# Row-halved projections in a four-layer attention kernel: one job in two half-wide banks instead of two jobs in two whole banks

## The chip, the cores and the metric

The kernel runs on one core of a Trainium2 chip. Its metric is the device time of one execution in microseconds (us), lower is better. Matrix products run on TensorE (PE, with its weight loads listed as PEld), elementwise work on VectorE (DVE), ScalarE (ACT) and GpSimd (POOL), and SyncE (SP) issues nearly all transfers (DMAs). Products land in PSUM, which has eight banks of 512 fp32 columns for 128 partitions; from there DVE or ACT copies them to SBUF.

## What is computed

An input of 2048 tokens by 512 features passes four residual layers, A, B, A, B. Each one normalizes its input, projects it, attends with 32 heads of 16 features, and projects back. All is fp32.

```python
def _A_ref(x, wqkv, w_phi, wo):        # linear attention on learned features
    q, k, v = qkv[0], qkv[1], qkv[2]
    phi_q = concatenate([softmax(q @ w_phi), softmax(-q @ w_phi)]); phi_k likewise
    kv = phi_k^T v;  z = sum phi_k
    return ((phi_q kv) / (phi_q z + 1e-6)) @ wo

def _B_ref(x, wq, wk, wv, wo, beta):   # N = 4 segments of L = 512 tokens
    for s in range(N):
        qs, ks, vs = q[:, :, s], k[:, :, s], v[:, :, s]
        p = softmax(qs ks^T * scale + causal mask)
        a_mem = (phi(qs) M) / (phi(qs) z + 1e-6)      # phi(t) = t + 1 if t > 0 else exp(t)
        o = sigmoid(beta) * a_mem + (1 - sigmoid(beta)) * (p vs)
        M = M + phi(ks)^T vs;  z = z + sum phi(ks)
    return o @ wo

x = x + _A_ref(_layernorm(x), ...); x = x + _B_ref(_layernorm(x), ...); and both once more
```

## The kernel before

The products that need accuracy are made of fp32r operands split in a high and a low part: hi·hi, hi·lo and lo·hi, three matmuls for each 128 rows of the contraction. A projection of one token block or one column block of 128 contracts over 512 features, so over four chunks `kc`.

**Layer B** (class `LayerB`) takes some 440 us of the span each time, and the change is there alone. Its method `steps` writes out the order of work by hand. It runs through 160 *slots* `k`, five for each of the 32 half blocks `m` (`R = 5`; a segment has eight half blocks, a half block has four heads). I call the five slots of a half block a *turn* and name a slot by its place, "slot 2.3" being slot 3 of turn 2 of a segment, as the tables do. In a slot come, in this order on PE: one piece of `attend` (the logits of the current half block, bank pair `lg`, then one exponential over 1024 columns on ACT, then POOL's causal mask), one piece of `maxima` (the logits of a later half block, banks `mx` and `my`, reduced by DVE to row maxima `mxs`), in slots 0 and 2 `weighted` (the product with v, bank `pv`), and then whatever the table has for the slot. `held` keeps PE's instructions in the order of the program, and `Ordered` does so for the other engines and for SP.

The tables `FIRST` (segment 0), `GAPS` (segments 1 and 2), `LAST` and `FINAL` (segment 3 of the two B layers) say what a slot does. `u/2` stands for two *units* of the projections, `max` for `put_maxima` (a PE transpose of `mxs` into a `g` bank, ACT's copy `mt`, and its DMA into row 63 of the queries that the logits read, `e<-mt` in the profile), `ln` for one 128-token block of the next segment's normalized input turned by four PE transposes (`columns`), `t` for four transposes of the features of k (`tokens`), `m` for the memory's update, `a` for its reading, `x` and `w` for loads. A `~` puts DVE's part of an end off to the next slot.

PSUM is full: two banks for `lg`, one each for `mx`, `my` and `pv`, and **three `g` banks** (`G = 3`), which the projections, the transposes and the memory's products share.

**Projections in the steps.** `PAIRS` names them two by two: q and k of a column block, v of a token block, and the output product `out` of the segment before. `pair` runs both jobs of a name pair at once, each in a whole `g` bank of 512 columns. The array is split in two halves of 64 rows; in one step job 0 uses rows 0 to 63 and job 1 rows 64 to 127 of the same chunk, and after the four chunks they swap ("turned"). A unit is one step: three matmuls of 64 rows by 512 columns for each job, eight units to the pair. Since the other half of the rows then adds to the same bank, the first matmul after the swap waits for a tick: `passed` has DVE copy one element (`beat`) after the last matmul of the half before, at the start of the next slot. Eight projections per B layer, early ones, are done whole by `whole` with all 128 rows (`BEFORE`); 52 per layer go through `pair`.

When a pair is complete, each job's end runs. For q and k that is `projected`: ACT copies the high part out of PSUM (tile `ta`), DVE subtracts it from the bank to give the low part (`ta<-g,ta`), and, where the features are wanted (q in segments 1 to 3, k in segments 0 to 2), ACT reads the bank again for exp (`self.later`, so a slot later) and for relu (another slot later in segments 0 and 1); POOL then makes the features of both. The bank is free after the last of these reads. For v, ACT copies the bank (`v<-g`); for `out`, DVE adds it to the residual (`xr<-g,xr`).

Weights of q and k come from DRAM by SP in halves of 64 rows into a ring of two places (`queue_w`). `stack` lays high and low parts of q and k out as operands of the logits with six DMAs (`e<-ta`): in slot 0 of a turn for `m < 4` and in slot 2 for later half blocks, three turns ahead.

Of the kernel before, what the change touches and what calls it, by code (L numbers as in the profile page):

```python
# [7 lines left out]
F32 = mybir.dt.float32  # L8
# [69 lines left out]


FIRST = """  # L80
0.1 u/2 | 0.2 max u/2 | 0.3 u/2 | 0.4 u/2~
1.0 m0 t1 u/1 | 1.1 u/2 | 1.2 max u/1 w | 1.3 u/2 | 1.4 u/2~
2.0 m1 ln | 2.1 ln~ | 2.2 max ln | 2.3 ln~ w | 2.4 w
3.0 t2 | 3.1 u/2 w | 3.2 max | 3.3 u/2 | 3.4 u/2
4.0 m2 | 4.1 u/2 load | 4.2 max | 4.3 u/2 | 4.4 u/2
5.0 n t3 | 5.1 u/2 | 5.2 max | 5.3 u/2~ n | 5.4 u/2
6.0 m3 n | 6.1 u/2 | 6.2 max | 6.3 u/2 | 6.4 a0+ u/2~
7.0 n t0+ u/1 | 7.1 u/2 | 7.2 n max u/1 | 7.3 u/2 n | 7.4 u/2~
# [12 lines left out]
LAST = """  # L101
0.0 u/1 | 0.1 u/2 | 0.2 n max u/1 | 0.3 u/2 n | 0.4 a1 u/2~ n
1.0 n u/1 | 1.1 u/2 n | 1.2 n max u/1 | 1.3 u/2 n | 1.4 u/2~ n
2.0 ln | 2.2 ln max | 2.3 u/3 | 2.4 a2 u/2 x0 x1 pre
3.0 ln u/1 | 3.1 u/1 | 3.2 ln max u/1 | 3.3 pre u/2 x2 | 3.4 u/2
4.1 x3 u/2 | 4.2 max | 4.3 pre u/2 | 4.4 a3 v/2
5.1 v/2 | 5.2 max v/1 | 5.3 fin v/1 | 5.4 v/2 pre
6.1 v/2 | 6.2 max | 6.3 fin v/2 | 6.4 v/2
7.1 pt p/3 v/2 | 7.2 v/2 | 7.3 fin v/2 p/3 | 7.4 p/3
"""  # L110
FINAL = """
0.0 u/1 | 0.1 u/2 | 0.2 max u/1 | 0.3 u/2 | 0.4 a1 u/2~
1.0 u/1 | 1.1 u/2 | 1.2 max u/1 | 1.3 u/2 | 1.4 u/2~
2.2 max | 2.3 u/3 pre | 2.4 a2 u/2 x0
3.0 x1 u/1 | 3.1 u/1 | 3.2 max u/1 | 3.3 pre u/2 x2 | 3.4 u/2
4.1 x3 u/2 | 4.2 max | 4.3 pre u/2 | 4.4 a3
5.2 max | 5.3 fin | 5.4 pre
6.2 max | 6.3 fin
# [9 lines left out]
def interleave_kernel(ctx, tc, x_in, a_wqkv, a_wphi, a_wo, b_wq, b_wk, b_wv, b_wo, b_beta,  # L128
# [15 lines left out]
    def nm(s):  # L144
        uid[0] += 1
        return f"{s}_{uid[0]}"
# [84 lines left out]
    def dma(out, in_):  # L231
        return sync.dma_start(out=out.bitcast(F32), in_=in_.bitcast(F32))
# [798 lines left out]
    class LayerB:  # L1031
# [22 lines left out]
        def values(self, s):  # L1054

            v = sp.tile([P, 4, VROW], F32, tag="v", bufs=2, name=nm("v"))
            self.vv[s] = [v]
            for j in (0, 2 * VW - 1):
                pool.memset(v[:, :, 0 : H * VW].rearrange("p t (h e) -> p t h e", e=2 * VW)[:, :, :, j : j + 1], 1.0)
            pool.memset(v[:, :, H * VW : H * VW + 1], 1.0)  # L1060
            hT = self.hT[s]
            for t in (0, 3, 1, 2):
                def end(po, t=t):
                    act.copy(v[:, t, 0 : H * VW].rearrange("p (h e) -> p h e", e=2 * VW)[:, :, 1 : 2 * VW - 1],
                             po.rearrange("p (h e) -> p h e", e=2 * DH))
                yield (lambda a, kc, t=t: hT[a][:, kc, t * P : (t + 1) * P], lambda b, kc: self.wv[b][:, kc, :],
                       end, lambda h: None)

        def queue_w(self, n, h):

            if n < len(self.wnext):
                m, c = self.wnext[n]
                rows = slice(64 * h, 64 * h + 64)
                dma(self.ring[rows, n % 2], wqk[m][rows, c])

        def whole(self, job):

            lhs, rhs, end, used = job
            po = PS("g", G)
            yield from mm3(po, lhs, rhs)  # L1080
            used(0)
            used(1)
            end(po)
            yield

        def pair(self, names, make):

            jobs = [make(n) for n in names[:2]]  # L1090
            po = [PS("g", G) for _ in jobs]
            order = [(0, 0), (0, 1), (0, 2), (0, 3), (1, 0), (1, 1), (1, 2), (1, 3)]
            if names[2:]:
                order = [(0, 0), (0, 1), (0, 2), (1, 0), (1, 1), (1, 2), (1, 3), (0, 3)]
            halves = [[0, 0], [0, 0]]
            for step, (turned, kc) in enumerate(order):
                for n, (a, b) in enumerate(((0, 0), (0, 1), (1, 0))):
                    for j, (lhs, rhs, _, _) in enumerate(jobs):
                        h = (j + turned) % 2
                        rows = slice(64 * h, 64 * h + 64)  # L1100
                        i = mm(po[j], lhsT=lhs(a, kc)[rows], rhs=rhs(b, kc)[rows], start=(step == 0 and n == 0),
                               stop=(step == 7 and n == 2), tile_position=(64 * h, 0))
                        if step and n == 0 and turned != order[step - 1][0]:
                            marked(i)
                        if j and n == 2 and step < 7 and turned != order[step + 1][0]:
                            last_half[0] = i
                for j, job in enumerate(jobs):
                    h = (j + turned) % 2
                    halves[j][h] += 1
                    if halves[j][h] == NC:  # L1110
                        job[3](h)
                if step == 7:
                    for p, job in zip(po, jobs):
                        job[2](p)
                yield

        def proj(self, s, c, m):

            d, hT = self.st.setdefault((s, c), {}), self.hT[s]
            n = self.wused  # L1120
            w = self.ring[:, n % 2]
            self.wused += 1
            return (lambda a, kc: w[:, a, kc, :], lambda b, kc: hT[b][:, kc, :],
                    lambda pp: self.projected(d, s, m, pp), lambda h: self.queue_w(n + 2, h))

        def projected(self, d, s, m, pp):

            hi, lo = d["part", m] = [T2("ta1", TA, F32R) for _ in range(2)]
            act.copy(hi, pp)
            wait(lambda: dve.tensor_tensor(out=lo, in0=pp, in1=hi.bitcast(F32), op=SUB))  # L1130
            if not (s == 0 if m == 0 else s == NSEG - 1):
                e = d["phi", m] = T2("tb2", TB2)
                r = T2("tb3", 2)

                def first():
                    act.activation(e, pp, AF.Exp)

                def second():
                    act.activation(r, pp, AF.Relu)
                    pool.tensor_scalar(e, e, 1.0, None, op0=MIN)  # L1140
                    pool.tensor_tensor(out=e, in0=e, in1=r, op=ADD)
                self.later += [first, (lambda: self.later.append(second)) if s < 2 else second]

        def at(self, k, f, *a):

# [351 lines left out]

        def out(self, s):
            for t in range(4):
                def end(po, t=t):  # L1500
                    def added():
                        x = self.xq.pop(0)
                        dve.tensor_tensor(out=x, in0=po, in1=x, op=ADD)
                        sync.dma_start(out=self.xdst[4 * s + t], in_=x)
                    wait(added)
                yield (lambda a, kc, t=t: self.oT[s, kc][a][:, t * P : (t + 1) * P],
                       lambda b, kc: self.wo[b][:, kc, :], end, lambda h: None)

        def early(self):

# [20 lines left out]
        def opening(self):  # L1531
            self.wo = []
            self.wnext = [(m, c) for _ in range(NSEG) for c in range(NC) for m in range(2)]
            self.ring = wp.tile([P, 2, 2, NC, P], F32R, tag="w4", bufs=1, name=nm("wqk"))
            self.wused = 0
            for n in range(2):
                for h in range(2):
                    self.queue_w(n, h)
                yield
            self.wv = []  # L1540
            yield from bring(self.wv, "bwv")
# [7 lines left out]
        def steps(self, side, after, table_end):  # L1549
# [20 lines left out]

            def units():
                for s in range(NSEG):
                    for names in PAIRS[0 if s == 0 else 1 if s < NSEG - 1 else 2]:
                        yield from self.pair(names.split(), lambda name: job(name, s))
            units = units()

            def do(what, s, k):
# [186 lines left out]
```

## Time and profile before

| | us |
|---|---|
| median of 3 runs | 1469.98 (1467.95 to 1474.74) |
| the profiled execution | 1470.59 |
| its span | 1468.9 |
| busy of the span: PE / DVE / ACT / POOL | 1381.1 / 976.4 / 816.2 / 736.9 |

One execution was profiled. The span runs from its first to its last instruction; the profiled execution's own time is 1.7 us longer and lies 0.6 us above the median. Busy time is the union of an engine's instructions; matmuls are pipelined and their ends are modelled, so PE's busy time holds some waiting too. "PEclk" is the share of TensorE's full clock that was granted.

The two B layers' steps lie at 293 to 735 us and at 1012 to 1455 us of the span. The matmuls of the row-halved projections are listed by shape as 64*128 (rows by columns of weights), 64x512 (rows by columns that stream).

### The profile page before, as it was taken

Reading aid. Unit: us, or ns where it says so; the run is one execution under the profiler, and the core shown is the slowest. Engines: PE = TensorE matmul, PEld = TensorE weight load, DVE = VectorE, ACT = ScalarE, POOL = GpSimd, SP = SyncE. Lnnn points to the kernel's source line nnn. Section 1 sums busy time; section 2 is a strip of 40 time slices with the busy share of each in tenths; the row PEclk is TensorE's granted clock in tenths of the full one; section 3 lists DMA queues with packets and bytes.
Section 4 is the critical chain, followed back from the end, with each engine's and each line's share of the span. In section 5 each row is a group of like instructions: output and inputs, shape, how many; then the busy total and the mean of one; then the engine's idle time right before and its main releaser. Section 6 shows DMA issues by size and latency. Waiting matters only on the chain. (4 is left out here: it accounts for less than half of the span.)

```text
span 1468.9 us, 35919 instructions
## 1 busy us (share of the span) xinstructions
PE 1381.1 (94%) x13318; PEld 998.7 (68%) x13318; DVE 976.4 (66%) x3088; ACT 816.2 (56%) x1244; POOL 736.9 (50%) x1073
## 2 busy tenths in 40 slices
PE   9999999998999899988999999999999988998998
PEld 7787787765666565655568887876566666666654
DVE  5766896875666566567646778958666665666673
ACT  5655455355775675556644434543567656755653
POOL 1678764134564555544524456531355456644543
PEclk9999999998999999999999999999999999999998
DMA  5469285555665575657640106754655566655551
GB/s 190 128 218 360 81 274 171 161 134 144 155 142 155 143 167 135 156 147 209 174 153 33 55 23 201 224 169 119 169 145 136 135 164 163 147 145 140 145 167 60
DMA packets 136766, 225.46 MB, mean 153 GB/s; under 512 B 22352, under 2 KB 40912, under 8 KB 136592
## 3 DMA queue, kind: packets, MB, share of 16 engines
q1 hardware_dynamic: 135488, 222.91, 54.5%
q8 instruction: 107, 1.75, 0.5%
q14 instruction: 67, 0.55, 0.1%
q10 hardware_dynamic: 1104, 0.24, 0.1%
HBM read 116.39 MB, written 43.25 MB: 109 GB/s over the span
## 5 line engine op out<-in xcount | busy, mean ns | idle before, releaser
L203 ACT ACTIVATE P<-lg 128x1024 f32<-128x1024 f32 x316 | 324.9, 1028 | 226.4 <-PE lg L225 163.4
L203 POOL TENSOR_SCALAR_AFFINE_SELECT P<-P 128x256 f32<-128x256 f32 (+1 forms) x448 | 191.5, 442 | 452.7 <-ACT P L203 449.5
L225 PE MATMUL g<-hh,wqk 64*128 64x512 f32 (+1 forms) x944 | 299.8, 410 | 18.6 <-ACT tb L203 6.2
L203 DVE CUSTOM_DVE_ANT_0 junk<-mx,mask 128x128 uint8<-128x128 f32 (+2 forms) x384 | 147.3, 421 | 126.7 <-PE my L225 77.4
L225 PE MATMUL g<-w,hh 64*128 64x512 f32 (+1 forms) x656 | 221.8, 415 | 0.3 <-ACT hh L203 0.3
L225 PE MATMUL g<-w,oh 64*128 64x512 f32 (+1 forms) x700 | 194.3, 417 | 4.7 <-ACT tb L203 4.2
L225 PE MATMUL lg<-e,e 64*128 64x512 f32 (+1 forms) x1010 | 163.0, 349 | 31.7 <-DMA e<-mt 17.2
L225 PEld LDWEIGHTS g<-hh,wqk 64*128 64x128 f32 (+1 forms) x944 | 156.0, 188 | 48.4 <-ACT tb L203 10.3
L225 PE MATMUL pv<-P,v 128*32 128x512 f32 (+3 forms) x2048 | 175.5, 462 | 1.5 <-ACT ot L203 1.5
L225 PE MATMUL g<-hl,wqk 64*128 64x512 f32 (+1 forms) x472 | 162.4, 398 | 0.0
L225 PE MATMUL my<-e,e 63*128 63x256 f32 (+3 forms) x519 | 150.5, 350 | 5.5 <-DVE mxs L203 5.2
L225 PEld LDWEIGHTS lg<-e,e 64*128 64x128 f32 x1010 | 106.1, 189 | 71.3 <-ACT P L203 28.1
L225 PE MATMUL mx<-e,e 63*128 63x256 f32 (+3 forms) x519 | 151.3, 343 | 2.0 <-DVE mxs L203 1.4
L203 DVE CUSTOM_DVE_ANT_0 junk<-my,mask 128x128 uint8<-128x128 f32 (+2 forms) x384 | 146.7, 420 | 0.1
L203 DVE CUSTOM_DVE_ANT_0 mx<-mx,mask 128x512 f32<-128x512 f32 x128 | 89.3, 697 | 71.3 <-PE mx L225 37.3
L225 PEld LDWEIGHTS g<-w,hh 64*128 64x128 f32 (+1 forms) x656 | 118.8, 189 | 19.8 <-issue 2.5
L225 PE MATMUL g<-w,hl 64*128 64x512 f32 (+1 forms) x328 | 129.6, 395 | 0.0
L225 PEld LDWEIGHTS pv<-P,v 128*32 128x32 f32 x2048 | 54.9, 113 | 106.9 <-issue 94.9
L225 PEld LDWEIGHTS g<-w,oh 64*128 64x128 f32 (+1 forms) x700 | 103.0, 188 | 31.3 <-issue 8.2
L225 PE MATMUL g<-w,ol 64*128 64x512 f32 (+1 forms) x350 | 115.5, 393 | 2.6 <-DVE ol L203 2.6
L225 PEld LDWEIGHTS my<-e,e 63*128 63x128 f32 (+1 forms) x519 | 92.2, 190 | 24.7 <-DVE mxs L203 5.7
L225 PEld LDWEIGHTS mx<-e,e 63*128 63x128 f32 (+1 forms) x519 | 95.3, 190 | 14.3 <-DVE mxs L203 5.2
(191 smaller groups left out, 2937.1 us busy)
## 6 DMA issues: line engine op xcount, KB each, us to landing
e<-ta SPq DMA_DIRECT2D x384, 128.0 KB
wqk<-wqk SPq DMA_DIRECT2D x128, 256.0 KB
x<-x SPq DMA_DIRECT2D x48, 256.0 KB
xr<-x SPq DMA_DIRECT2D x32, 256.0 KB
x<-xr SPq DMA_DIRECT2D x28, 256.0 KB
tmp<-U SPq DMA_DIRECT2D x56, 128.0 KB
KN<-inv SPq DMA_DIRECT2D x28, 256.0 KB
pq<-tb SPq DMA_DIRECT2D x24, 256.0 KB
```

Of the source, the lines that this page charges most:

```text
L203: i = f(*a, **k)
L225: return held(nc.tensor.matmul(*a, **k))
```

## The change

`pair` becomes `split`: one job alone, in two `g` banks of which only 256 columns are used. Columns 0 to 255 go to bank 0 with rows 0 to 63 of each chunk while columns 256 to 511 go to bank 1 with rows 64 to 127; after four chunks the halves swap rows. A unit is now three matmuls of 64 rows by 256 columns for each of the two banks, eight units to the job, and each table entry `u/4` is half a job. Every half job must end in one slot and the other begin in a later one, since `passed` issues the tick at the start of a slot.

The ends change with it. `summed` copies both banks out at once, half on ACT and half on DVE, and all later reads are of that copy in SBUF: the high part on ACT, exp and relu on ACT (all three in the next slot), and the low part on POOL instead of DVE. v is copied half by ACT and half by DVE; `out` is added by DVE in two halves. `~` is gone.

Jobs are dealt anew: `JOBS` in place of `PAIRS`, four units in slots 0, 1, 3 and 4 of most turns. `max` moves from slot 2 to slot 0 (same half block, so two slots earlier), right behind the last piece of that half block's maxima; in `GAPS` and `FIRST` the `m`, `t` and `ln` of a slot 0 stay ahead of it. The two `ln` of slot 2.2 are put in slots 2.2 and 2.3 of `GAPS`. `stack` is in slot 0 for all half blocks. Weights come as one DMA of twice the size per job, issued when a job ends, into one of two tiles.

```diff
 GAPS = """
-0.0 u/1 | 0.1 u/2 | 0.2 n max u/1 | 0.3 u/2 | 0.4 a1 u/2~
-1.0 m0 t1 n n u/1 | 1.1 u/2 | 1.2 n max u/1 | 1.3 u/2 | 1.4 u/2~
-2.0 m1 ln | 2.2 ln max ln | 2.3 u/3 | 2.4 a2 u/2 x0 x1
-3.0 ln u/1 | 3.1 u/1 | 3.2 max t2 u/1 | 3.3 u/2 x2 | 3.4 u/2
-4.0 m2 u/1 | 4.1 u/3 load | 4.2 max u/1 | 4.3 u/3 x3 | 4.4 a3 u/3
-5.0 n t3 u/1 | 5.1 u/3 | 5.2 max u/1 | 5.3 u/2 n | 5.4 u/2
-6.0 m3 u/1 | 6.1 u/3 | 6.2 max u/1 | 6.3 u/3 | 6.4 a0+ u/2
-7.0 n n t0+ | 7.1 u/2 begin | 7.2 n max | 7.3 u/2 n N | 7.4 u/2~ N
+0.0 max u/4 | 0.1 u/4 | 0.2 n | 0.3 u/4 | 0.4 a1 u/4
+1.0 m0 t1 n n max u/4 | 1.1 u/4 | 1.2 n | 1.3 u/4 | 1.4 u/4
+2.0 m1 ln max | 2.2 ln | 2.3 ln u/3 | 2.4 a2 u/3 x0
+3.0 ln max | 3.1 u/1 x1 | 3.2 t2 u/1 | 3.3 u/4 | 3.4 u/4
+4.0 m2 max u/4 | 4.1 u/4 load | 4.2 u/4 | 4.3 u/4 x2 | 4.4 a3 u/4
+5.0 n t3 max u/4 | 5.1 u/4 x3 | 5.2 u/4 | 5.3 u/4 n | 5.4 u/4
+6.0 m3 max u/4 | 6.1 u/4 | 6.2 u/4 | 6.3 u/4 | 6.4 a0+ u/4
+7.0 n n t0+ max u/4 | 7.1 u/4 begin | 7.2 n u/4 | 7.3 u/4 n N | 7.4 u/4 N
 """
...
 FIRST = """
-2.0 m1 ln | 2.1 ln~ | 2.2 max ln | 2.3 ln~ w | 2.4 w
-3.0 t2 | 3.1 u/2 w | 3.2 max | 3.3 u/2 | 3.4 u/2
+2.0 m1 ln max | 2.2 ln | 2.3 w | 2.4 w
+3.0 ln max | 3.1 w | 3.2 t2 ln | 3.3 u/4 | 3.4 u/4
...
-PAIRS = (("v3 k2", "q3 k3", "q0+ k0+", "v0+ q1+", "v1+ k1+", "v2+ q2+"),
-         ("v3 k2", "q3 k3", "out out /", "q0+ out", "k0+ out", "v0+ q1+", "v1+ k1+", "v2+ q2+"),
-         ("v3 k2", "q3 k3", "out out /", "out out"))
+JOBS = ("k2 v q3 k3 q0+ k0+ v+ q1+ k1+ v+ q2+ k2+",
+        "v v q3 k3 out/ q0+ k0+ out out q1+ k1+ out v+ v+ q2+ k2+",
+        "v v q3 k3 out/ out out out")
...
+        def split(self, job, late=False):
+            lhs, rhs, _, end = job
+            po = [PS("g", G)[:, 0:256] for _ in range(2)]
+            order = [(p, kc) for p in range(2) for kc in range(NC)]
+            if late:
+                order.append(order.pop(NC - 1))
             for step, (turned, kc) in enumerate(order):
                 for n, (a, b) in enumerate(((0, 0), (0, 1), (1, 0))):
-                    for j, (lhs, rhs, _, _) in enumerate(jobs):
+                    for j in range(2):
                         h = (j + turned) % 2
                         rows = slice(64 * h, 64 * h + 64)
-                        i = mm(po[j], lhsT=lhs(a, kc)[rows], rhs=rhs(b, kc)[rows], start=(step == 0 and n == 0),
-                               stop=(step == 7 and n == 2), tile_position=(64 * h, 0))
+                        i = mm(po[j], lhsT=lhs(a, kc)[rows], rhs=rhs(b, kc)[rows, 256 * j : 256 * j + 256],
+                               start=(step == 0 and n == 0), stop=(step == 7 and n == 2), tile_position=(64 * h, 0))
...
+            def summed(p0, p1):
+                self.queue_w()
+                hi, lo = parts()
+                x = lo.bitcast(F32)
+                act.copy(x[:, 0:256], p0)
+                dve.tensor_copy(x[:, 256:512], p1)
+                def low():
+                    pool.tensor_tensor(out=lo, in0=x, in1=hi.bitcast(F32), op=SUB)
+                def high():
+                    act.copy(hi, x)
+                    if not wanted:
+                        low()
...
+                def features():
+                    high()
+                    act.activation(e, x, AF.Exp)
+                    act.activation(r, x, AF.Relu)
+                    low()
                     pool.tensor_scalar(e, e, 1.0, None, op0=MIN)
                     pool.tensor_tensor(out=e, in0=e, in1=r, op=ADD)
+                self.later.append(features)
...
                 if op == "max":
-                    if (k + LEAD) // R <= N:
-                        self.put_maxima((k + LEAD) // R - 1)
+                    if (k + LEAD + 1) // R <= N:
+                        self.put_maxima((k + LEAD + 1) // R - 1)
...
-                if k % R == (0 if m < 4 else 2) and 0 <= m < N:
+                if k % R == 0 and 0 <= m < N:
                     self.stack(m)
```

`FIRST`, `LAST` and `FINAL` are dealt in the same way: `max` in slot 0, `u/4` where `u/2` was or half a job spread over slots 2.3 to 3.2.

More of the change, by code (lines that the diff above doesn't have):

```diff
@@ L1106, in pair @@
                             last_half[0] = i
[L1107 to L1111, printed above, removed]
                 if step == 7:
-                    for p, job in zip(po, jobs):
-                        job[2](p)
+                    end(*po)
                 yield
         def proj(self, s, c, m):
-            d, hT = self.st.setdefault((s, c), {}), self.hT[s]
@@ L1120, in proj @@
[L1120 to L1139, printed above, removed]
+            d, hT, w = self.st.setdefault((s, c), {}), self.hT[s], self.w4.pop(0)
@@ new lines, in proj, with parts, end, first @@
+            wanted = not (s == 0 if m == 0 else s == NSEG - 1)
+            def parts():
+                d["part", m] = [T2("ta1", TA, F32R) for _ in range(2)]
+                if wanted:
+                    d["phi", m] = T2("tb2", TB2)
+                return d["part", m]
+            def end(pp):
+                self.queue_w()
+                hi, lo = parts()
+                act.copy(hi, pp)
+                wait(lambda: dve.tensor_tensor(out=lo, in0=pp, in1=hi.bitcast(F32), op=SUB))
+                if wanted:
+                    e, r = d["phi", m], T2("tb3", 2)
+                    def first():
+                        act.activation(e, pp, AF.Exp)
+                    def second():
+                        act.activation(r, pp, AF.Relu)
+                        pool.tensor_scalar(e, e, 1.0, None, op0=MIN)
+                        pool.tensor_tensor(out=e, in0=e, in1=r, op=ADD)
+                    self.later += [first, (lambda: self.later.append(second)) if s < 2 else second]
@@ new lines, in summed @@
+            def summed(p0, p1):
+                self.queue_w()
+                hi, lo = parts()
+                x = lo.bitcast(F32)
[7 more added lines that the diff above has]
+                        low()
+                if not wanted:
+                    self.later.append(high)
+                    return
+                e, r = d["phi", m], T2("tb3", 2)
+                def features():
[3 more added lines that the diff above has]
+                    low()
@@ L1533, in opening @@
             self.wnext = [(m, c) for _ in range(NSEG) for c in range(NC) for m in range(2)]
[L1534 to L1538, printed above, removed]
+            self.w4 = []
+            for _ in range(2):
+                self.queue_w()
                 yield
@@ L1572, in units @@
                 for s in range(NSEG):
-                    for names in PAIRS[0 if s == 0 else 1 if s < NSEG - 1 else 2]:
-                        yield from self.pair(names.split(), lambda name: job(name, s))
+                    for name in JOBS[0 if s == 0 else 1 if s < NSEG - 1 else 2].split():
+                        yield from self.split(job(name.rstrip("/"), s), name[-1] == "/")
             units = units()
```

90 lines of the change are left out of this document (43 added, 47 removed).

## Prediction, made before the change was run

> **What bounds the kernel now.** The page first: how long, and which engine is full.
>
> ```profile
> span 1468.9 us, 35919 instructions
> PE 1381.1 (94%) x13318; PEld 998.7 (68%) x13318; DVE 976.4 (66%) x3088; ACT 816.2 (56%) x1244; POOL 736.9 (50%) x1073
> ```
>
> PE is the bound, and it must be asked whether it streams or waits. The windows of the two B layers' steps, the only stretches that the change touches (columns: length, then busy time of PE, PEld, DVE, ACT, POOL, granted clock, DMA share, GB/s):
>
> ```profile
> 293.00:735.00 442.00, 407.63 (x3874) 274.29 (x3873) 282.18 (x1112) 274.66 (x391) 224.49 (x366) 0.97 0.60 155
> 1012.00:1455.00 443.00, 408.65 (x3873) 272.37 (x3872) 277.42 (x1097) 270.29 (x384) 225.32 (x363) 0.96 0.56 143
> ```
>
> Some 34 us of each are idle and the clock is 3 to 4% low, though it is full elsewhere. So there is something to win that is not arithmetic. The waits of PE (total, times, longest) say where:
>
> ```profile
> PE lg L225 <- DMA e<-mt: 17.2, 12, 4.2
> PE lg L225 <- ACT P L203: 14.5, 27, 1.6
> PE g L225 <- ACT tb L203: 10.9, 13, 2.2
> PE my L225 <- DVE mxs L203: 5.2, 24, 0.3
> PE g L225 <- ACT mmq L203: 4.4, 2, 2.2
> PE g L225 <- DVE ta L203: 3.9, 6, 1.0
> PE g L229 <- ACT mt L203: 3.0, 4, 0.8
> PE g L225 <- DVE ol L203: 2.6, 5, 0.8
> PE g L225 <- DVE xr L203: 2.5, 2, 1.2
> PE g L229 <- DVE mem L203: 2.3, 6, 0.4
> ```
>
> Two families matter: logits that wait for the maxima's row (`e<-mt`, 17.2 us), and projections or transposes that wait for a `g` bank which ACT or DVE still reads. PE's timeline in slot 4.3 of segment 0 shows the second kind as a pair opens:
>
> ```profile
> 356.98 0.49 PE L225 MATMUL g<-w,hh 64*128 64x512 f32 x1
> 359.66 0.79 PE L225 MATMUL g<-hh,wqk 64*128 64x512 f32 x1 [2.19 <-ACT tb L203]
> ```
>
> One bank was free, the other came 2.7 us later, and the matmul is then 0.79 us long instead of 0.39: the clock has dropped. Windows laid on four of the eleven drops in the steps, the first and the last among them, and on a slot without projections before one:
>
> ```profile
> 334.10:340.90 6.80, 6.58 (x32) 3.24 (x32) 3.24 (x14) 2.19 (x3) 0.81 (x2) 0.50 0.75 215
> 433.10:439.90 6.80, 6.58 (x37) 4.03 (x38) 2.98 (x8) 3.31 (x6) 6.63 (x7) 0.50 0.49 118
> 641.30:644.70 3.40, 3.40 (x23) 1.51 (x24) 2.86 (x7) 1.88 (x3) 2.24 (x3) 0.50 0.80 224
> 1433.20:1440.00 6.80, 6.70 (x40) 2.31 (x39) 2.11 (x8) 2.98 (x4) 1.80 (x4) 0.50 0.35 109
> 430.40:432.10 1.70, 0.83 (x7) 0.49 (x6) 1.70 (x6) 1.56 (x3) 0.00 (x0) 1.00 1.00 205
> ```
>
> Nine drops last 6.8 us and two 3.4, all at half clock: 34 us if PE is the bound in them. Three follow the waits above: one of 6.8 in each layer behind slot 4.3 of segment 0, and the 3.4 at 641.3 behind the 4.2 us wait for `mt`. The others follow stretches thin in matmuls, like slot 2.1 (PE busy 0.83 of 1.70).
>
> **What goes.** *The mt wait.* `max` comes two slots sooner, so the row has five slots instead of three; a slot is 442 / 160 = 2.8 us, the longest wait 4.2 us. All 17.2 us go; next late is ACT's exponential of the slot before. In SP's queue the `e<-mt` still stands behind the six `e<-ta` of its slot, since `stack` moves with it; those may now hold SP until the logits of the slot before are done, a wait under a slot, against five.
>
> *Bank waits.* The waits tb, mmq, ta and xr are 10.9 + 4.4 + 3.9 + 2.5 = 21.7 us. A job's banks are now free after one half-wide copy on each engine:
>
> ```profile
> L203 ACT CAST ta<-oh 128x256 fp32r<-128x256 f32 x8 | 3.3, 426 | 2.2 <-POOL P L203 1.7 <-DMA awo<-ta 0.5
> L203 DVE TENSOR_TENSOR kva<-my,kva 128x256 f32<-128x256 f32 x8 | 3.3, 418 | 0.8 <-PE my L225 0.8
> L203 ACT ACTIVATE tb<-g 128x512 f32<-128x512 f32 x96 | 53.6, 604 | 3.0 <-DVE ta L203 3.0
> L203 ACT CAST ta<-g 128x512 fp32r<-128x512 f32 x64 | 36.7, 589 | 37.0 <-PE g L225 37.0
> L203 DVE TENSOR_TENSOR ta<-g,ta 128x512 fp32r<-128x512 f32 x64 | 43.5, 690 | 64.7 <-ACT ta L203 54.2 <-ACT tb L203 10.0
> L203 POOL TENSOR_TENSOR ol<-tmp,oh 128x512 fp32r<-128x512 f32 x28 | 36.1, 1289 | 0.9 <-ACT oh L203 0.9
> L203 DVE COPY beat<-bd 1x1 f32<-1x1 f32 x58 | 7.9, 137 | 27.8 <-PE g L225 27.8
> ```
>
> About 0.42 us on each, side by side, instead of 0.59 + 0.69 + 0.60 + 0.60 with up to two slots between. But two banks are wanted anew for every job, and in slot 0 `m`, `t` and `max` want one each as well, of three. I take three quarters, 16 us (between 0 and 22). Of the transposes' 3.0 + 2.3 I take 3, since no pair holds two banks for five slots any more.
>
> *Clock.* The three drops behind these waits: half of 6.8 + 6.8 + 3.4, 8.5 us. Sum of the gains: 17.2 + 16 + 3 + 8.5 = **44.7 us**.
>
> **What comes.** *Streaming.* These rows count the jobs, at 16 hi matmuls each, 54 + 26 + 24 = 104:
>
> ```profile
> L225 PE MATMUL g<-hh,wqk 64*128 64x512 f32 x864 | 273.2, 411 | 17.1 <-ACT tb L203 6.2 <-ACT mmq L203 4.4 <-DVE ta L203 3.9
> L225 PE MATMUL g<-w,hh 64*128 64x512 f32 x416 | 145.3, 423 | 0.0
> L225 PE MATMUL g<-w,oh 64*128 64x512 f32 x384 | 89.7, 422 | 4.2 <-ACT tb L203 4.2
> ```
>
> With the lo ones 24 each, 2496 matmuls and loads of 512 columns, or 1248 side by side in pairs. They become 2496 pairs of 256 columns, with twice the loads. Half-wide pairs stand already in the logits and maxima (PE's timeline):
>
> ```profile
> 527.78 0.39 PE L225 MATMUL g<-hh,wqk 64*128 64x512 f32 x1
> 528.01 0.45 PE L225 MATMUL lg<-e,e 64*128 64x256 f32 x4
> 528.30 0.28 PE L225 MATMUL my<-e,e 63*128 63x256 f32 x1
> 528.60 0.39 PE L225 MATMUL g<-w,hh 64*128 64x512 f32 x1
> ```
>
> Starts count: 0.23 us for 512 columns, 0.29 for the logits' 256 + 384 (their row is named by its first), 0.30 for the maxima's 256 + 384. Times 512 / 640 that is 0.232 and 0.240, so two half pairs cost 2 to 10 ns more than a whole one, 2 to 13 us over 1248. I take 4, nearer to the first.
>
> [...]
>
> *Maxima sooner.* The transposes of `max` now stand on PE right behind the reduction that they read, and all later work of the slot behind them. A slot 0 of before:
>
> ```profile
> 520.70 0.40 PE L225 MATMUL my<-e,e 63*128 63x512 f32 x1
> 521.70 0.73 DVE L203 CUSTOM_DVE_ANT_0 my<-my,mask 128x512 f32<-128x512 f32 x1
> 522.24 0.50 PE L225 MATMUL g<-w,hh 64*128 64x512 f32 x1
> 522.35 0.14 DVE L203 DVE_READ_ACCUMULATOR2_ANT mxs<- 128x1 f32 x1
> ```
>
> PE is ready at 522.24, the maxima at 522.49: 0.3 us late. Where `m`, `t` or `ln` stand between, that is covered. Bare are six slots of segments 0 to 2, five of `LAST` and seven of `FINAL`: 18 x 0.3 = 5 us; nothing, if DVE is early, or 59 if it comes 0.95 late in all 62 turns.
>
> *ACT.* For the 44 jobs with features, high part, exp and relu come in one go, about 1.8 us, where exp and relu stood in slots of their own. The next exponential over `lg` is behind them, and PE's logits two slots on. ACT is busy 275 of 442 us, some 1.0 us a slot free, so 1.8 spill little: 0.15 us each, 6 us (0 to 13).
>
> *At nothing.* DVE loses 54 subtractions of 0.69 (37 us) and gets 80 half copies at 0.42, 24 split additions (+0.15 each) and 52 more ticks of 0.14: 34 + 4 + 7, even. The swapped matmul waits for its tick, behind it all PE; the logits and maxima of the slot stand ahead of it, and PE shows no wait for a tick now (0 to 10 us if DVE is late). POOL gets 54 subtractions of 1.29 us, 70 us, in half a span of idle time; the masks behind them have slots to spare, and `stack` wants the parts two slots later (0 to 5). Weights: 64 DMAs of 512 KB for 128 of 256, asked for two jobs ahead, with SP waiting for the job's end as before.
>
> *Clock again.* The thin stretch grows: segment 0 has no projection from slot 2.0 to 3.2, and `GAPS` but two half units from 3.0 to 3.2. I take three new drops, in slots that ACT binds anyway, at 2 us of 3.4: 6 us (0 to 24). [...]
>
> Costs: 4 + 5 + 6 + 6 = 21. **Sum:** 1470.6 - 44.7 + 21 = 1446.9; forecast **1447 us**. This execution is 0.6 above the median, so I correct nothing.
>
> **Rivals.** *Everything gives*: all bank waits (21.7 + 5.3) and all eleven drops (34) go with the 17.2: -78 + 15 = 1407. For it: the even dealing. Against: slot 2.1 stays empty.
> *The banks aren't free sooner*: ACT's copy stands behind an exponential and the feature burst, and the openings collide with `t` and `max`. Only mt (17.2) and its drop (1.7) are won, and 21 paid: 1473. For it: `tb` heads the bank waits already.
> *Slower: the maxima hold PE.* If DVE, which now also copies at the end of each job, enters slot 0 late, each of 62 transposes waits 0.95 us, 59 in place of 5: 1501. It cancels the gain from about 0.5 us each. Against: DVE is busy 64% of the steps.
> *Slower: loads bind.* The loads' row:
>
> ```profile
> L225 PEld LDWEIGHTS g<-hh,wqk 64*128 64x128 f32 x864 | 140.9, 188 | 42.5 <-ACT tb L203 9.9 <-DVE ta L203 6.6 <-ACT mmq L203 5.6
> ```
>
> 1248 more of them side by side, unhidden at 0.188 us, are 235 in place of 4: 1678. Against: the starts above.
>
> **Chances.** Forecast 0.54 (alone 1427 to 1465), everything gives 0.14, no bank gain 0.17, maxima 0.13, loads 0.02. A measurement can tell some 0.5% from no change, here 1463 to 1477. Faster: 0.51 of the forecast, 0.14, and 0.03 of the third: 0.68. Same: 0.03 + 0.11 + 0.01. Slower: 0.03 + 0.12 + 0.02. The range, 1407 to 1487, leaves out the far half of the first rival, most of the maxima's and the loads'.
>
> **What would show it.** Right: no `e<-mt` among PE's waits; no `g` wait over 1 us outside slot 0; no drop at slot 4.3 of segment 0; half-wide projection pairs 0.115 to 0.12 us apart; DVE `mxs` as a small new releaser of `g`. Wrong: `g <- DVE mxs` over 20 us, more than eleven drops, logits waiting for ACT well over 14.5 us, or pairs more than 0.13 apart.

## The result, and the profile after

| | median, us | ratio to before, 95% interval |
|---|---|---|
| before, 11 runs on the same chip | 1468.96 (1463.34 to 1474.74) | |
| changed kernel, 11 runs | 1478.7 (1475.08 to 1485.64) | 1.0068 [1.0047, 1.0088] |

The change makes the kernel 10 us slower; the forecast was 1447, some 23 faster. The profiled execution took 1475.08 us, the shortest of the eleven, so its rows show a little less than the median lost. Its page and the windows of the two stretches of steps (columns as in the prediction):

```profile
span 1473.0 us, 41101 instructions
PE 1380.3 (94%) x15814; PEld 1055.6 (72%) x15814; DVE 981.2 (67%) x3190; ACT 831.8 (56%) x1298; POOL 799.5 (54%) x1127
```

```profile
291.00:748.00 457.00, 419.58 (x5174) 309.96 (x5173) 288.20 (x1173) 287.74 (x427) 258.71 (x397) 0.97 0.55 153
1013.00:1456.00 443.00, 405.32 (x5095) 298.74 (x5094) 279.35 (x1145) 276.89 (x410) 256.81 (x389) 0.97 0.52 144
```

The first window is longer than the one shown of before only because the kernel before has logits until 746.5 us too, beyond the 735 at which that window was closed. In the same stretches it has (before):

```profile
291.00:748.00 457.00, 422.54 (x3960) 283.78 (x3957) 288.56 (x1132) 281.15 (x401) 226.99 (x371) 0.97 0.59 154
1013.00:1456.00 443.00, 408.65 (x3871) 272.50 (x3871) 276.45 (x1093) 269.47 (x383) 225.78 (x363) 0.96 0.56 143
```

PE's busy time over the whole span is what it was (1381.1). POOL has 62.6 us more of it, all in the steps: 31.7 and 31.0 in the two stretches. The waits of PE in the changed kernel:

```profile
PE lg L225 <- ACT P L203: 31.6, 42, 1.8
PE pv L225 <- ACT ot L203: 17.6, 12, 3.6
PE g L229 <- DVE hl L203: 7.0, 5, 1.4
PE g L229 <- DVE mxs L203: 6.6, 12, 2.3
PE g L229 <- ACT tb L203: 4.1, 6, 0.7
PE g L225 <- ACT tb L203: 3.5, 11, 0.6
```

Against the list of before: `e<-mt` (17.2) is gone, and of the bank waits of the projections (tb 10.9, mmq 4.4, ta 3.9, xr 2.5) a tb of 3.5 is left. So what the change was to remove, it removed. New is `pv <- ACT ot` (17.6, before 1.5), and `lg <- ACT P` has doubled, from 14.5. The transposes (L229) wait longer too: 11.1 us for a bank that DVE or ACT still reads (hl 7.0 and tb 4.1; before mt 3.0, mem 2.3 and hl 1.4, 6.7 together), and 6.6 us for the reduction that they read (mxs), a wait that before doesn't have.

**The new wait of 3.6 us, followed back.** It is in slot 5.0 of segment 1. The changed kernel's PE, ACT and POOL there (timelines: start, length, engine, instruction, and in brackets the idle time before it and its releaser):

```profile
475.31 2.15 PE L225 MATMUL pv<-P,v 128*32 128x512 f32 x12 [3.60 <-ACT ot L203]
...
468.63 1.02 ACT L203 ACTIVATE P<-lg 128x1024 f32<-128x1024 f32 x1 [0.77 <-PE lg L225]
473.97 0.62 ACT L203 CAST oh<-tmp 128x512 fp32r<-128x512 f32 x1 [4.32 <-POOL tmp L203]
474.49 0.68 ACT L203 ACTIVATE ot<-pv,bd 68x512 f32<-68x512 f32 x1
...
467.86 1.30 POOL L203 TENSOR_TENSOR ta<-ta,ta 128x512 fp32r<-128x512 f32 x1
469.11 1.51 POOL L203 TENSOR_SCALAR tb<-tb 128x512 f32<-128x512 f32 x1
470.70 1.29 POOL L203 TENSOR_TENSOR tb<-tb,tb 128x512 f32<-128x512 f32 x1
471.93 0.77 POOL L203 TENSOR_SCALAR_AFFINE_SELECT P<-P 128x256 f32<-128x256 f32 x2
472.67 1.27 POOL L203 TENSOR_TENSOR tmp<-tmp,ot 128x512 f32<-128x512 f32 x1
```

Read from the bottom. POOL runs without a gap; its last row is `joined`, the addition of the two parts of an output. ACT's next instruction in order is that output's copy (`oh<-tmp`), so ACT stands 4.32 us although other work is behind it. That work is the copy `ot<-pv,bd` that frees the one `pv` bank, and PE waits for the bank. The first row of POOL is the change's subtraction; without its 1.30 us, and the one a job earlier, `joined` would end sooner. The same place before:

```profile
471.31 1.28 POOL L203 TENSOR_TENSOR tmp<-tmp,ot 128x512 f32<-128x512 f32 x1
...
472.12 1.02 ACT L203 ACTIVATE P<-lg 128x1024 f32<-128x1024 f32 x1 [1.62 <-PE lg L225]
473.04 0.61 ACT L203 CAST oh<-tmp 128x512 fp32r<-128x512 f32 x1
```

There the copy follows the exponential with no wait. From the two traces I had three suspects: POOL's lateness, the maxima's transposes in slot 0, and ACT's feature burst; and with them the cost of twice as many matmuls.

Of the runs that follow, experiment 7 has two of six executions at 3193 and 6693 us, which no trace here explains; its time is the median of the other four.

### The profile page after: what moved, and what is told of

The parts are those of the page before. It is cut to its first block, busy times and chain, and to the rows that moved or that the text cites. A ratio compares the mean times of both kernels' runs of the same rounds, so it can differ in the third digit from the quotient of the medians.

```text
span 1473.0 us, 41101 instructions
## 1 busy us (share of the span) xinstructions
PE 1380.3 (94%) x15814; PEld 1055.6 (72%) x15814; DVE 981.2 (67%) x3190; ACT 831.8 (56%) x1298; POOL 799.5 (54%) x1127
## 4 chain that ended last, share of the span: by engine, by line
PE 69%; ACT 9%; POOL 8%; DVE 7%; issue 3%; DMA 3%; SPq 1%; ACTq 0%; DVEq 0%; POOLq 0%
PE g L225 42%; PE pv L225 9%; PE lg L225 5%; PE g L229 4%; PE mx L225 3%; ACT P L203 3%; PE my L225 3%; POOL tb L203 2%; ACT tb L203 2%; POOL P L203 2%; POOL tmp L203 2%; PE lg L229 1%; POOL ta L203 1%; ACT ta L203 1%; DVE es L203 1%
## 5 line engine op out<-in xcount | busy, mean ns | idle before, releaser
L225 PE MATMUL g<-hh,wqk 64*128 64x256 f32 (+1 forms) x1808 | 214.8, 290 | 3.6 <-ACT tb L203 2.9
L225 PE MATMUL pv<-P,v 128*32 128x512 f32 (+3 forms) x2048 | 182.3, 464 | 18.0 <-ACT ot L203 17.6
L225 PEld LDWEIGHTS g<-hh,wqk 64*128 64x128 f32 (+1 forms) x1808 | 177.1, 186 | 19.1 <-ACT tb L203 5.4
L225 PE MATMUL g<-w,oh 64*128 64x256 f32 (+1 forms) x1084 | 188.0, 334 | 0.5 <-ACT hh L203 0.4
L225 PE MATMUL lg<-e,e 64*128 64x512 f32 (+1 forms) x1010 | 157.8, 353 | 31.6 <-ACT P L203 31.6
L225 PE MATMUL g<-hl,wqk 64*128 64x256 f32 (+1 forms) x904 | 160.9, 287 | 0.7 <-DVE hl L203 0.7
L225 PE MATMUL g<-w,hh 64*128 64x256 f32 (+1 forms) x1072 | 159.8, 316 | 0.2 <-ACT hh L203 0.2
L225 PEld LDWEIGHTS g<-w,oh 64*128 64x128 f32 (+1 forms) x1084 | 124.0, 189 | 25.4 <-issue 9.9
L225 PEld LDWEIGHTS lg<-e,e 64*128 64x128 f32 x1010 | 91.6, 189 | 65.6 <-ACT P L203 55.9
L225 PE MATMUL g<-w,ol 64*128 64x256 f32 (+1 forms) x542 | 125.5, 317 | 1.0 <-DVE ol L203 0.7
L225 PEld LDWEIGHTS g<-hl,wqk 64*128 64x128 f32 (+1 forms) x904 | 114.1, 186 | 2.5 <-DVE hl L203 1.1
L225 PE MATMUL g<-w,hl 64*128 64x256 f32 (+1 forms) x536 | 110.2, 304 | 0.0
```

The source lines that it names most:

```text
L225: return held(nc.tensor.matmul(*a, **k))
```

## The experiments

All ratios are to the kernel before, run on the same chip beside the variant; where two variants are compared in us, it is the difference of their ratios times 1469, and by the intervals such a difference is good to some 4 us.

### One part undone at a time

**1. `low` on DVE.** POOL is rid of the subtraction.

```diff
-                    pool.tensor_tensor(out=lo, in0=x, in1=hi.bitcast(F32), op=SUB)
+                    dve.tensor_tensor(out=lo, in0=x, in1=hi.bitcast(F32), op=SUB)
```

> The changed kernel (1478.7 us, +9.7 over before), with the low part of q and k subtracted by DVE again instead of POOL. Theory POOL (the 54 subtractions of 1.3 us and the features that go with them make POOL late, ACT waits in order for POOL's `tmp` before `oh<-tmp`, and bank pv and the logits wait for ACT): PE's waits pv <- ACT ot fall from 17.6 us to under 5, the whole to 1455 to 1465. Rival ACT (the burst of high part, exp and relu is what holds the logits): 1474 to 1482, lg <- ACT P stays near 31 us. Rival streaming or maxima: 1475 to 1482 as well. DVE could give some of it back, with 54 x 0.75 us more work.

Measured: 1492.41 us, 1.0159 [1.0134, 1.0184], slower still. The two rows of PE's waits that tell why, and one of DVE's and one of ACT's:

```profile
PE pv L225 <- ACT ot L203: 1.4, 2, 0.7
PE g L225 <- DVE beat L203: 10.7, 10, 1.1
...
DVE ta L203 <- ACT tb L203: 56.9, 44, 2.3
...
ACT oh L203 <- POOL tmp L203: 4.4, 9, 1.6
```

With POOL relieved, ACT's wait for `tmp` falls from 28.9 us to 4.4 and PE's for `pv` from 17.6 to 1.4, as the theory has it. But the subtraction writes over its own input, so on DVE it waits for exp and relu (56.9 us in 44 jobs), and the tick of the swap stands behind it: PE waits for `beat`, up to 1.1 us at a time, and another 5.4 us for it ahead of `my`. These 16 us take back what `pv` gained; why the kernel is slower still, by 13 us, these rows don't show. The time missed both expectations; DVE was the wrong place to try this.

**2. The burst in two slots.**

```diff
-                def features():
+                def first():
                     high()
                     act.activation(e, x, AF.Exp)
+
+                def second():
                     act.activation(r, x, AF.Relu)
                     low()
...
-                self.later.append(features)
+                self.later += [first, lambda: self.later.append(second)]
```

> The changed kernel with high part and exp in the slot after the job, and relu, low part and POOL's two feature operations one slot later, in place of all in one slot. Rival ACT: lg <- ACT P falls from 31.6 to 18 us or less and the time to 1460 to 1468. Theory POOL: POOL's work is the same and comes a slot later still, so pv <- ACT ot stays over 12 us or grows, and the time is 1470 to 1485.

Measured: 1501.69 us, 1.0235 [1.0209, 1.026], the slowest of all. POOL's three instructions now come a slot later, and `joined` behind them:

```profile
ACT oh L203 <- POOL tmp L203: 53.1, 23, 6.5
```

That is 28.9 us in the changed kernel and 2.0 before; PE's `pv <- ACT ot` grows with it, from 17.6 to 33.6. The time is above both expectations, nearer to theory POOL. Most of the further 25 us are seen in the clock: the mean granted clock is 0.967 over these five executions and 0.981 over the changed kernel's eleven, which is some 20 us of full clock.

**3. The maxima's transposes back in slot 2,** all else as changed. `max` goes from every `.0` cell of the tables to the `.2` cell:

```diff
-0.0 max u/4 | 0.1 u/4 | 0.2 n | 0.3 u/4 | 0.4 a1 u/4
+0.0 u/4 | 0.1 u/4 | 0.2 max n | 0.3 u/4 | 0.4 a1 u/4
...
-                    if (k + LEAD + 1) // R <= N:
-                        self.put_maxima((k + LEAD + 1) // R - 1)
+                    if (k + LEAD) // R <= N:
+                        self.put_maxima((k + LEAD) // R - 1)
```

> The changed kernel with only the maxima's transposes put back to slot 2 of the turn. If their move gained what the prediction says (the 17.2 us of e<-mt), that wait comes back in part: 1484 to 1497, with e<-mt over 8 us among PE's waits. Rival maxima (the transposes hold PE behind their own reduction): 1465 to 1474, PE g <- DVE mxs (6.6 us) gone and no e<-mt wait.

Measured: 1466.87 us, 0.9999 [0.9979, 1.0018]: 10 us come back, as the rival said. And `e<-mt` doesn't:

```profile
PE lg L225 <- DMA e<-mt: 2.1, 3, 1.0
```

So the transposes' move costs 10 us, and it isn't what removed the 17.2 us. What they wait for is seen in slot 3.0 of segment 1 of the changed kernel (PE, then DVE):

```profile
443.76 0.66 PE L229 MATMUL g<-ident,x 128*128 128x128 f32 x4
445.82 0.28 PE L229 MATMUL g<-ident,mxs 128*16 128x128 f32 x1 [1.40 <-DVE hl L203]
...
443.73 0.14 DVE L203 DVE_READ_ACCUMULATOR2_ANT mxs<- 128x1 f32 x1
445.07 0.69 DVE L203 TENSOR_TENSOR hl<-g,hh 128x512 fp32r<-128x512 f32 x1 [1.21 <-ACT hh L203]
```

The maxima are ready at 443.87. The transpose starts 1.95 us later, when DVE has read `ln`'s product out of its bank: the open job holds two of the three `g` banks, `ln` the third, and `max` is the fourth user.

**4. The kernel before with half-wide matmuls,** each 512 columns of a pair in two matmuls of 256 into the same bank, no other change.

```diff
+                    for part, j, (lhs, rhs, _, _) in [(x, j, job) for x in range(2) for j, job in enumerate(jobs)]:
+                        cut = slice(256 * part, 256 * part + 256)
...
-                        i = mm(po[j], lhsT=lhs(a, kc)[rows], rhs=rhs(b, kc)[rows],
+                        i = mm(po[j][:, cut], lhsT=lhs(a, kc)[rows], rhs=rhs(b, kc)[rows, cut],
```

> The kernel BEFORE, with each 512-column matmul of a pair issued as two of 256 columns into the same bank, so twice as many matmuls and weight loads and nothing else. Starts of half pairs were 0.120 us apart in the changed kernel, of whole ones 0.232 before. Rival streaming: 2496 x 4 ns = +8 to +14 us over before, 1477 to 1483. The prediction's price: +4, 1471 to 1475. If loads bind anywhere: over 1490.

Measured: 1478.25 us, 1.0057 [1.0031, 1.0082], so 8 us (5 to 12), as the rival said. The changed kernel's PE shows the spacing:

```profile
356.93 0.28 PE L225 MATMUL g<-w,hl 64*128 64x256 f32 x2
357.05 0.40 PE L225 MATMUL g<-w,hh 64*128 64x256 f32 x4
357.29 0.28 PE L225 MATMUL g<-w,hl 64*128 64x256 f32 x2
```

Between the two rows `hl` lie three pairs and 0.36 us: 0.120 each, 8 ns more for two than the whole pair's 0.232, and 8 x 1248 is 10 us. The clock has a part in the time as well: the mean granted clock is 0.976 over these eight executions and 0.979 over the nineteen of before, some 5 us of full clock. Which share of the 8 us is spacing and which is clock, no run separates.

### POOL's order, and both losses together

**5. `joined` earlier,** ahead of the job's subtraction in POOL's order. This tests POOL's lateness without burdening another engine.

```diff
-JOIN = (..., ((9.5, 9.5, 11.5, 12, 13.5),) * 4, ((9.5, 10.5, 12.5, 13, 13.5),) * 4)
+JOIN = (..., ((9.5, 9.5, 10, 12, 13.5),) * 4, ((9.5, 10.5, 11, 13, 13.5),) * 4)
```

> The changed kernel with one edit: the addition that joins the two halves of an output stands one and a half slots earlier in POOL's order, ahead of the job's subtraction, minimum and addition instead of behind them. Theory (POOL's new subtraction makes that addition late, ACT waits for it and PE for ACT): ACT's waits of oh for POOL tmp fall from 28.9 us to under 5, PE's waits of pv for ACT ot from 17.6 to under 4, and the time is 14 to 20 us below the changed kernel's 1478.7: 1459 to 1465. Rival (the feature burst on ACT itself costs the time, POOL only shows it): the waits move to lg behind ACT P, and the time stays within 4 of the changed kernel, 1475 to 1483.

Measured: 1466.54 us, 0.9994 [0.9979, 1.0009]: 11 us come back, and `pv <- ACT ot` leaves the list of PE's waits. The same place in its trace (POOL, ACT):

```profile
469.23 1.29 POOL L203 TENSOR_TENSOR tmp<-tmp,ot 128x512 f32<-128x512 f32 x1
470.47 1.30 POOL L203 TENSOR_TENSOR ta<-ta,ta 128x512 fp32r<-128x512 f32 x1
...
470.01 1.02 ACT L203 ACTIVATE P<-lg 128x1024 f32<-128x1024 f32 x1 [0.78 <-PE lg L225]
470.93 0.61 ACT L203 CAST oh<-tmp 128x512 fp32r<-128x512 f32 x1
```

The order is turned round, and ACT's copy follows its exponential as before the change. ACT's waits of `oh` for `tmp` fall from 28.9 us to 9.2, not quite the 5 that was expected, and the time is 1.5 us above the expected stretch; the mechanism is as expected. The new place costs 5.7 us of `pv` waiting for POOL's masks, which now stand behind the addition.

**6. Both:** experiments 3 and 5 in one kernel.

> The changed kernel with two edits: the maxima's transposes back in slot 2 (1466.9 alone) and the joining addition earlier in POOL's order. Theory (two separate losses): the gains add up, 1447 to 1454, faster than the kernel before. Rival (the two stalls cover each other, one comes up when the other goes): 1460 to 1467.

Measured: 1453.32 us, 0.9914 [0.9895, 0.9932], faster than before by 13 us. The two gains, 10 and 11, make 21, and both together gave 23: within the intervals they add up, so these are separate losses.

### What made the maxima's row late

Experiment 3 left this open. `stack`'s six copies and the row go through one queue, SP's. Before, in turn 7 of segment 2 (SP, then ACT):

```profile
633.19 4.55 SPq L203 DMA_DIRECT2D e<-ta  x6
638.23 0.33 SPq L203 DMA_DIRECT2D inv<-dn  x1
638.65 0.60 SPq L203 DMA_DIRECT2D e<-mt  x1
...
632.53 0.25 ACT L203 ACTIVATE mt<-g 16x128 fp32r<-16x128 f32 x1
```

The row is ready at 632.78 and issued 5.9 us later, behind the copies. That is the wait of 4.2 us.

**7. The kernel before, `stack` one slot later,** so that its copies come behind the row.

```diff
-                if k % R == (0 if m < 4 else 2) and 0 <= m < N:
+                if k % R == (0 if m < 4 else 3) and 0 <= m < N:
```

> The kernel before with one edit: from the fifth unit on, stack stands in slot 3 instead of slot 2, so its six copies come behind the row of the maxima in SP's queue and not ahead of it. Theory (the row was late because stack's copies stood ahead of it in the queue; with the maxima in slot 2 the row has time enough): lg behind e from mt falls from 17.2 us to under 4, and the time to 1449 to 1456. Rival (as predicted: three slots are too few for the row, wherever stack stands): the wait stays over 12 us and the time at 1465 to 1471.

Measured: 1483.85 us (1481.39 to 1488.06), 1.0108 [1.0087, 1.0128], which neither expected. PE's waits:

```profile
PE mx L225 <- DMA e<-ta: 21.1, 18, 3.5
...
PE lg L225 <- DMA e<-mt: 2.8, 2, 2.3
```

The row's wait falls from 17.2 us to 2.8, but now the operands are late for the maxima's own products. One slot later is too late for `stack`.

**8. The kernel before, `max` in slot 0,** nothing else: the edit of 3 the other way, in the tables of before.

```diff
-1.0 m0 t1 n n u/1 | 1.1 u/2 | 1.2 n max u/1 | 1.3 u/2 | 1.4 u/2~
+1.0 m0 t1 n n max u/1 | 1.1 u/2 | 1.2 n u/1 | 1.3 u/2 | 1.4 u/2~
```

> The kernel before with one edit: the maxima's transposes stand in slot 0 as in the changed kernel, all else as it was. As predicted: lg behind e from mt goes (-17 us), the transposes wait for their own reduction in bare slots (+5), so 1455 to 1459. Theory after the first runs (they cost about 12): mxs stands among the releasers of g and of the transposes with 6 us or more, and the time is 1461 to 1467.

Measured: 1473.61 us, 1.0044 [1.0026, 1.0063], a loss of 6 where the prediction's steps give a gain of 12, and above the theory's stretch too. `e<-mt` is gone, though `stack` is where it was. In its place stand waits of the transposes, 28.7 us in three rows, the first two for a bank (19.6) and the third for their own reduction:

```profile
PE g L229 <- DVE mem L203: 9.8, 18, 1.2
PE g L229 <- DVE hl L203: 9.8, 7, 1.4
PE g L229 <- DVE mxs L203: 9.1, 9, 3.9
```

**12. Experiment 6 with `stack` back in slot 2** from the fifth unit on, as before the change; `max` is in slot 2 in both.

```diff
-                if k % R == 0 and 0 <= m < N:
+                if k % R == (0 if m < 4 else 2) and 0 <= m < N:
```

> The kernel with both edits (1453.3 us, lg behind e from mt 4.4 us; its maxima's transposes stand in slot 2, as before) with one part of the change undone: from the fifth unit on, stack again in slot 2, so that its six copies come ahead of the maxima's row in SP's queue. Theory (it is stack's place, not that of the maxima's transposes, that made the row late): lg behind e from mt rises to 12 us or more, and the time by 8 or more, to 1461 to 1470. Rival (the row came sooner because the banks and the copies are free sooner): the wait stays under 7 us and the time within 4 of 1453.

Measured: 1476.52 us, 1.0051 [1.0037, 1.0065], 20 us slower than experiment 6 and 6.5 above the expected stretch. One place in turn 5 of segment 1, first in 12, then in 6 (SP):

```profile
486.94 3.94 SPq L203 DMA_DIRECT2D e<-ta  x6
490.98 0.62 SPq L203 DMA_DIRECT2D inv<-dn  x1
491.70 0.60 SPq L203 DMA_DIRECT2D e<-mt  x1
```

```profile
480.82 3.79 SPq L203 DMA_DIRECT2D e<-ta  x6
...
489.96 0.58 SPq L203 DMA_DIRECT2D e<-mt  x1
```

In 6 the copies are long through when the row comes. Its wait is 11.1 us in 12 and 4.4 in 6, a little less than expected, and only a third of the loss: the mean granted clock falls as well, from 0.984 of 1458.2 us to 0.977 of 1477.3, which is 34.0 - 23.3 = 10.7 us of full clock. So with `max` in slot 2 it is `stack`'s move to slot 0, a by-part of the change, that keeps the row on time. With `max` in slot 0, as in the changed kernel, that move isn't needed for it: experiment 8 has `stack` in its old place and no such wait.

### ACT's burst

With POOL and the maxima out of the way, the burst was tried again, on experiment 6.

**9. relu, `low` and POOL's rest a slot later** (the edit of 2). **10. The high part in the slot in which the job ends,** exp and relu in the next. **11. Both: one step a slot.**

> The kernel with both edits (1453.3 us) and one more: relu, with POOL's work behind it, one slot after high part and exp. Theory (U and the feature burst stand between two exponentials of the logits and hold the next logits): lg behind ACT P falls from 35.9 us to about 22 (0.6 us each in some 24 turns) and the time to 1438 to 1448. Rival (what counts is when POOL gets its part, as the first run of this edit suggested): ACT's waits of oh for POOL tmp rise from 9.9 us to over 20 and the time to 1455 to 1475.

> The kernel with both edits and one more: the high part is copied in the slot in which the job ends, right behind the two half copies, so that exp and relu alone are left for the next slot. Theory (the burst holds the next logits): lg behind ACT P falls from 35.9 us to about 22 and the time to 1438 to 1448; POOL's part is no later. Rival (ACT waits there for DVE's half copy, and the exponential behind it comes late instead): lg behind ACT P stays over 32 and the time within 4 of 1453.

> The kernel with both edits, the high part in the slot in which the job ends, exp one slot later and relu with POOL's work two slots later: one step of ACT a slot. Theory (the burst holds the next logits): lg behind ACT P under 14 us, about what the kernel before has, and the time 1430 to 1444. Rival (POOL's lateness counts more): ACT's waits of oh for POOL tmp over 20 us and the time 1453 to 1475.

```diff
+                act.copy(hi, x)
+
-                def features():
-                    high()
+                def first():
                     act.activation(e, x, AF.Exp)
+
+                def second():
                     act.activation(r, x, AF.Relu)
                     low()
...
-                self.later.append(features)
+                self.later += [first, lambda: self.later.append(second)]
```

| | us | ratio to before | `lg <- ACT P`, us | ACT `oh <- tmp`, us |
|---|---|---|---|---|
| 6 | 1453.32 | 0.9914 [0.9895, 0.9932] | 35.9 | 9.9 |
| 9 | 1452.55 | 0.9873 [0.985, 0.9896] | 32.6 | 25.0 |
| 10 | 1454.93 | 0.9887 [0.9865, 0.9909] | 31.9 | 10.2 |
| 11 | 1451.67 | 0.9871 [0.9844, 0.9899] | 27.0 | 25.2 |

The theory missed in all three: the waits fell by 3 to 9 us, not 14 to 22. By the ratios they gain 4 to 6 us over 6, though all their intervals still touch its own, and by the times themselves the four lie within 3.3 us. So a gain isn't shown; in 9 and 11 some of it may be hidden, since ACT's wait for `tmp` rises there to 25 us. Experiment 11 has the shortest time here, but these runs don't set it apart from 6, 9 and 10. The edit of 9 cost 25 us in experiment 2 and nothing here: ACT waits for `tmp` in both, but PE's `pv <- ACT ot` is 4.7 us here and 33.6 there.

## Why the prediction was wrong

*The mt wait: the amount right, half of the cause seen.* It said that the wait goes because `max` comes two slots sooner. That alone is enough (8). But `stack`'s move alone is enough too: with `max` left in slot 2 the wait is 2.1 us (3), and with `stack` back in front of it 11.1 (12). What made the row late was the queue behind the six copies. The prediction priced `stack`'s move only as a possible small cost, and didn't see that with it `max` could have stayed where it was.

*The bank waits: about right.* Taken 16 of 21.7; in PE's list 3.5 are left. This part wasn't run alone.

*The transposes' bank waits: wrong sign.* Taken as a gain of 3; they rose from 6.7 us (mt, mem, hl) to 11.1 (hl, tb).

*The maxima, 5 us: a failed step.* It looked at when the reduction is done, counted the bare slots, and said "Where `m`, `t` or `ln` stand between, that is covered." In the bare slots it was about right: 6.6 us in 12 waits for `mxs`. The slots called covered are the dear ones: all of the 11.1 us stand there, behind `ln` (hl) and `t` (tb), where `max` finds no bank. The prediction had the fact in hand, that "`m`, `t` and `max` want one each as well, of three", and used it for the jobs only. Measured, bare and covered slots together: 10 us (3).

*POOL, at nothing (0 to 5): the step that failed most.* "70 us, in half a span of idle time; the masks behind them have slots to spare." The masks had; `joined`, also behind them, had none, and ACT is in order behind `joined`, with the release of the only `pv` bank behind that. Measured: 11 us (5).

*Streaming, 4 us of 2 to 13: too small, within its bounds.* By the spacing it is 10, and the whole run gave 8 with the clock's part in it (4): the maxima's pairs (10 ns per two), and not the logits', were the nearer row.

*ACT's burst, 6 us: open.* The ratios of 11 and 6 differ by 6 us, with intervals that touch, and their times by 1.7.

*The clock.* In the profiled pair the changed kernel's mean is 0.982 of 1473.0 us against 0.976 of 1468.9, so 26.5 us of full clock are lost in place of 35.3: a gain of 8.8, where 8.5 - 6 = 2.5 was taken. But the profiled execution of before was low in clock: the 38 executions of it beside experiments 1 to 8 have a mean of 0.980, the changed kernel's eleven 0.981. So the gain is rather 1 to 2 us, near what was taken. No drop is left at slot 4.3 of segment 0, as said (granted clock 1.00 from 338.6 to 447.8 us and from 1062.2 to 1171.4). There are more drops, the prediction's sign of being wrong: twelve in the steps for eleven; but nine of them last 3.4 us and three 6.8, together 51 us at half clock in place of 68.

*The sum.* The forecast's net was -24. POOL 11, the maxima 5 more and streaming 4 more bring it to -4. The measured difference is +10, which leaves some 14. (The profiled pair leaves as much: with 6 less for its clock the sum is -10, and it differs by +4.5, 1475.08 to 1470.59.) The rise of `lg <- ACT P` from 14.5 to 31.6 us is 17, of which 6 was priced as the burst. With the burst spread out the wait is still 27.0 (11), so the burst doesn't explain most of the rise. I take it that PE, freed of other waits, comes sooner to logits whose exponential sets the pace; that is argued from the rows, and no run shows it.

Of the two rivals that ended slower, one named the right place, the maxima, but with one wait of the two (DVE late; the larger one is the bank) and six times the price. The other, loads that bind, is ruled out by the spacing of 0.120 us. None named POOL, so the rivals had no form of what cost most. That 1479 us lies between 1407 and 1487 is no merit of the account: the forecast was a gain, and the range reached that far for rivals that didn't come true.

## What to carry to other kernels

Idle time of an engine says nothing of what stands behind an instruction in its order (on POOL, busy 50% of the span before, the added work cost 11 us here): before an operation goes to a half-idle engine, list every instruction behind it there and who waits for each, across two engines if the next one is in order too. When an operation is moved, count the buffers that are held in its new place, also where something "covers" its input (here the transposes waited 11.1 us for a bank). And look into the transfer queue at a late transfer: what was issued ahead of it may be cheaper to move than what feeds it (`stack` moved, the row's wait is 2.1 us in experiment 3, of 17.2 before).

## What was not expected of the hardware

In the changed kernel PE's clock halved behind PE's longest wait, and also where PE had no wait over 1.40 us. Windows of 3.4 us: the starts of two drops, and the window before the second (columns as above):

```profile
475.10:478.50 3.40, 3.19 (x20) 1.40 (x20) 0.00 (x0) 1.56 (x3) 1.65 (x2) 0.51 0.90 199
447.80:451.20 3.40, 3.40 (x22) 1.28 (x22) 2.80 (x10) 1.02 (x1) 1.04 (x3) 0.51 0.37 89
444.40:447.80 3.40, 1.54 (x16) 1.16 (x17) 1.62 (x8) 1.88 (x3) 0.14 (x1) 1.00 0.23 50
```

The drop at 475.1 follows PE's wait of 3.60 us: from 471.7 to 475.1 PE was busy for 0.02 us. The one at 447.8 follows a window in which PE was busy 1.54 of 3.40 us, with no wait over 1.40. PE's busy share in the window before doesn't sort these cases: in the same trace the drop at 1437.7 (granted clock 0.50) follows a window with 2.42 of 3.40 us busy (1434.3 to 1437.7), and a window with 1.84 of 3.40 (659.5 to 662.9) has full clock (1.00) in it and in the 3.4 us behind it. What sets off a drop is not shown by these windows.

The clock also goes with the spread of the times: twelve executions of experiment 3, one and the same kernel, lie between 1463.50 us (granted clock 0.984) and 1473.95 (0.975); the six below 1465 us have 0.982 to 0.984, the six above 1468 us 0.973 to 0.980.
